# Fourier mixing and an MLP mixer in one kernel: second sine table turned ahead of stage one, last carried products ahead of the first token layer, the first chunk's residual added in PSUM

## Chip, core and metric

The kernel runs on one core of a Trainium2 chip. The time is the device time of one execution in microseconds (us); several executions are timed and the median is quoted. A profile is of one further or one of these executions, on the hardware profiler, and its span is about 1.8 us shorter than the time of the same run. Engines: PE is TensorE's matmul, PEld its weight load, DVE VectorE, ACT ScalarE, POOL GpSimd, SP SyncE.

## The reference

```python
def _attn_ref(x):                       # x: (8, 3008, 256)
    X = np.fft.fft(x, axis=1)
    X = np.fft.fft(X, axis=2)
    return X.real.astype(np.float32)

def _moe_ref(x, w_tok1, w_tok2, w_ch1, w_ch2):
    xt = x.transpose(0, 2, 1)
    h = np.maximum(xt @ w_tok1, 0.0) @ w_tok2       # the token layer, 256 hidden
    u = x + h.transpose(0, 2, 1)                    # the token residual
    h2 = np.maximum(u @ w_ch1, 0.0) @ w_ch2         # the channel layer, 1536 hidden
    return (u + h2).astype(np.float32)

# reference: _moe_ref(_attn_ref(x), ...)
```

## The kernel before

The kernel makes sine tables, transforms batch 0 in a setup ("head") of some 33 us, and then runs a software pipeline over eight batches of six chunks of 512 tokens. Each chunk has four quarter-chunks ("subs"). In a quarter-chunk PE does three channel products `pc` (from `ut` and `wc1`), parts of the next batch's transform and token layer, and a quarter of the second channel layer of the chunk before (`px`, `py`, or `po` in plain chunks). DVE runs its instructions in program order here, so a wait of one instruction holds those behind it: the residual that stands behind the fold (explained below) in DVE's queue began at 47.12 us in the profile of before.

The head's order, with the parts that the change touches (cuts are marked `# ...`):

```python
    warm(24)
    table3(tq, vq, (shift0[:], shift1[:]))
    turn(tp, tts_p, 16)                     # 12 PE transposes, 2 ACT copies, 16 filler products
    table_d()
    pieces = fold0()
    take(pieces, 5)
    own = zw0()                             # stage one and two of batch 0
    take(own, 2)
    turn_rows(tts_p, 1.0, 0)
    # ...
    turned_out(tts_q, turn_in(tq))          # the second table turned, in the middle of stage one/two
    for g2, e in enumerate((1, 1)):
        carried(tts_p, hp, g2, e)           # hp, hq: w_tok1 carried through the transform
    # ...
    mirrored(state[0]["w"], ps_any("pt1"))
    own = front(0)
    carried(tts_q, hq, 1, 1)
    take(own, 1)                            # third(0): writes yt, the transform's chunk 0
    carried(tts_q, hq, 2, 0)
    take(own, 1)                            # token layer, part 0, both halves
    carried(tts_q, hq, 3, 1, ps_mm)
    carried(tts_q, hq, 4, 0, ps_mm)
    carried(tts_q, hq, 5, 0, ps_mm)
    take(own, 3)                            # token layer, part 1; then pu of chunk 0, two halves
    tables_folded()
    filler(12)
    load_wc2()
    if BB > 1:
        x_tiles[1] = load_x(1)              # xp (plain loads) and xm (two gathers) of batch 1
    early = fold(1, [nc.vector] * 4)
```

The token layer of batch 0 and the residual of a chunk:

```python
            pts = [ps_out("pt1") for _ in range(2)]
            for th in range(2):
                tok1(pts[th], th, 0)
            yield
            sqs = []
            for th in range(2):
                tok1(pts[th], th, 1)
                sqs.append(part_q(pts[th]))              # ACT copy
            uvs = [units(pts[th], sqs[th]) for th in range(2)]   # DVE: a copy, a subtract, an add
            relu(0, uvs[0], (0,))
            # ...
            for h in range(2):                           # per chunk
                # ... pu = two products of w_tok2 with uu
                nc.vector.tensor_tensor(
                    out=ut[:, h, 0:n].rearrange("p (a b) -> p a b", b=64),
                    in0=pu[:, 0:n].rearrange("p (b a) -> p a b", b=64),
                    in1=y.rearrange("p (a b) -> p a b", b=64), op=AT.add)
```

In the steady loop, batch 1's fold (DVE, reads `xm`) is taken early, in six quarter-chunks of batch 0, from the last one of the first chunk to the first one of the third:

```python
                take(own, own_plan[b > 0][sub])
                # ...
                if b == 0 and sub == 4:
                    weight_sums()                        # DVE, needs wc2
                # ...
                if b == 0 and 3 <= sub < 9:
                    take(early, 2)
                    if sub == 8:
                        x_tiles[2] = load_x(2)
```

## Time and profile before

| | before |
|---|---|
| time, median of the first three runs | 607.27 us (607.20 to 607.56) |
| span of the profile | 605.8 us |
| PE busy | 589.6 us, 97% |
| first channel product | at 32.91 us |
| gather of batch 1's xm seen by DVE | at 45.68 us |
| PE standing on DVE's `sb` and `osb` near 58 us | 1.20 us and 0.25 us |

From the page of the kernel before: the span; the line of busy us, share of the span and number of instructions; and the granted clock in tenths, in 40 equal slices.

```profile
span 605.8 us, 15712 instructions
...
PE 589.6 (97%) x6323; PEld 421.7 (70%) x6323; DVE 454.3 (75%) x1022; ACT 437.0 (72%) x983; POOL 148.5 (25%) x234
...
PEclk9999999999999999999999999999999999999999
```

The table of busy time by stretch of the kernel before; its columns are the stretch, its length, and for PE, PEld, DVE, ACT and POOL the busy us with the number of instructions, then the granted clock, the DMA share and GB/s.

```profile
33.00:45.60 12.60, 12.60 (x76) 6.44 (x74) 7.15 (x12) 9.66 (x18) 0.00 (x0) 1.00 1.21 173
45.60:59.20 13.60, 12.40 (x95) 7.96 (x94) 13.28 (x30) 8.53 (x16) 0.51 (x2) 1.00 0.54 107
...
100.00:300.00 200.00, 200.00 (x2148) 142.09 (x2146) 154.65 (x332) 146.92 (x336) 49.03 (x73) 1.00 0.49 90
300.00:580.00 280.00, 280.00 (x3048) 200.43 (x3046) 207.40 (x449) 202.25 (x462) 59.40 (x92) 1.00 0.40 79
```

The clock was granted in full (1.00 in every stretch shown). From 100 us on PE is busy in every microsecond (200.00 of 200 us, then 280.00 of 280). So what happens earlier should do little more than move the moment at which this stretch begins. Between 45.6 and 59.2 us it is DVE that is full (13.28 of 13.60 us), and PE is not.

The chain of waits of the first 60 us of the kernel before, in order of time (start, us, what):

```profile
6.20 7.65 DMA w1p<-in_moe_w_tok_dram
...
14.14 13.87 DMA w2s<-in_moe_w_tok_dram
...
30.12 15.43 DMA xm<-in_x_dram,ix
...
45.68 0.24 DVE xp L455
...
58.66 0.47 DVE sb L753
```

After its first 6 us this chain doesn't pass through the head's compute at all. It runs from load to load (a DMA line's duration is the time from its issue to its landing) to the gather of xm for batch 1, then through DVE.

The timeline of DVE (start, us, engine, line, operation, out<-in, form, and in brackets the idle time before it with what ended it), kernel before:

```profile
41.33 0.68 DVE L704 TENSOR_TENSOR ut<-pu,yt 128x512 f16<-128x512 f32 x1
45.68 0.23 DVE L455 TENSOR_TENSOR xp<-xp,xm 94x16 f16<-94x16 f16 x1 [3.67 <-DMA xm<-in_x_dram,ix]
...
58.58 0.54 DVE L753 TENSOR_TENSOR sb<-c 128x768 f16<-128x768 f16 x1
```

DVE finished a residual at 42.0 us and then stood 3.67 us on the gather, because the fold comes next in its queue. From then on it works without a break up to the `sb` at 58.58.

The timeline of PE, kernel before, same columns:

```profile
31.07 1.33 PE L696 MATMUL pu<-w2s,uu 128*128 128x512 f16 x4 [0.73 <-ACT uu L627]
32.24 0.83 PE L298 MATMUL filler<-ident 128*128 128x128 f16 x12
32.91 1.58 PE L736 MATMUL pc<-ut,wc1p 128*128 128x512 f16 x6
...
57.65 0.33 PE L777 MATMUL py<-wst,sb 128*128 128x128 f16 x3
59.18 0.68 PE L777 MATMUL py<-wst,sb 128*128 128x128 f16 x9 [1.20 <-DVE sb L753]
60.10 0.83 PE L777 MATMUL px<-wst,sb 128*128 128x128 f16 x12 [0.25 <-DVE osb L762]
```

The first three lines are the end of the head: the products `pu`, twelve fillers while DVE adds the residual, the first channel product. The last three show PE waiting for DVE's `sb` and `osb` near 58 us.

### The profile page before, as it was taken

How to read it: one execution, taken by the hardware profiler on the slowest of the kernel's cores; microseconds unless marked ns; L12 is line 12 of the kernel's file. 1: busy time of each engine (PE TensorE's matmuls, PEld its weight loads, DVE VectorE, ACT ScalarE, POOL GpSimd, SP SyncE). 2: the span in 40 equal slices, each digit the busy share in tenths (PEclk: the TensorE clock that was granted, in tenths of full speed). 3: DMA queues.
4: the chain of work that ended last, by engine and by line, in shares of the span. 5: the costliest groups of instructions: out<-in, count | busy, mean ns of one | idle time of the engine just before them, and what ended most of it. 6: DMA issues, size and time to landing. Idle time of an engine off the chain costs nothing.

```text
span 605.8 us, 15712 instructions
## 1 busy us (share of the span) xinstructions
PE 589.6 (97%) x6323; PEld 421.7 (70%) x6323; DVE 454.3 (75%) x1022; ACT 437.0 (72%) x983; POOL 148.5 (25%) x234
## 2 busy tenths in 40 slices
PE   5999999999999999999999999999999999999996
PEld 3855667666777677666777677766777677766675
DVE  8759699559886698667988689755979666766672
ACT  8775986777677767677767777677776877767772
POOL 7600414112242131402223211411221112111131
PEclk9999999999999999999999999999999999999999
DMA  9995945643457223662519332492231424242423
GB/s 152 210 177 117 176 62 97 141 62 63 53 107 155 57 54 88 134 88 54 97 44 178 70 80 63 83 173 53 54 85 44 86 53 88 55 70 62 87 60 99
DMA packets 86665, 56.53 MB, mean 93 GB/s; under 512 B 54928, under 2 KB 83536, under 8 KB 85840
## 3 DMA queue, kind: packets, MB, share of 16 engines
q1 hardware_dynamic: 78048, 37.84, 32.5%
q0 software_dynamic: 8320, 17.49, 16.9%
q8 instruction: 49, 0.80, 0.5%
q14 instruction: 24, 0.20, 0.1%
q10 hardware_dynamic: 224, 0.20, 0.1%
HBM read 34.98 MB, written 24.64 MB: 98 GB/s over the span
## 4 chain that ended last, share of the span: by engine, by line
PE 86%; DMA 6%; DVE 5%; issue 1%; ACT 1%; POOL 1%; DVEq 0%; POOLq 0%
PE pc L736 37%; PE px L777 23%; PE py L777 9%; PE pu L696 6%; PE po L834 3%; PE pt L604 3%; DMA xm<-in_x_dram,ix 3%; DMA w2s<-in_moe_w_tok_dram 2%; PE pz L509 1%; DMA w1p<-in_moe_w_tok_dram 1%; DVE sb L753 1%; PE pq L636 1%; PE py L636 1%; DVE osb L762 1%; DVE xp L457 1%
## 5 line engine op out<-in xcount | busy, mean ns | idle before, releaser
L739 ACT ACTIVATE c<-pc 128x512 f16<-128x512 f32 (+1 forms) x572 | 295.8, 593 | 38.2 <-PE pc L736 20.6
L762 POOL TENSOR_TENSOR osb<-osb,rt 128x256 f32<-128x256 f32 x84 | 81.2, 966 | 375.6 <-DVE osb L762 359.9
L736 PE MATMUL pc<-ut,wc1p 128*128 128x512 f16 x576 | 140.5, 379 | 0.0
L777 PEld LDWEIGHTS <-c 128*128 128x128 f16 x2016 | 121.4, 98 | 20.7 <-issue 1.3
L736 PE MATMUL pc<-ut,wc1m 128*128 128x512 f16 (+1 forms) x576 | 134.8, 370 | 0.0
L704 DVE TENSOR_TENSOR ut<-pu,yt 128x512 f16<-128x512 f32 (+1 forms) x96 | 64.7, 674 | 52.7 <-PE pu L696 52.7
L777 PEld LDWEIGHTS <-sb 128*128 128x128 f16 x1512 | 89.9, 98 | 12.5 <-DVE sb L753 2.1
L782 ACT ACTIVATE m<-px 128x256 f32<-128x256 f32 x126 | 48.6, 386 | 68.6 <-PE px L777 43.1
L736 PEld LDWEIGHTS <-wc1p 128*128 128x128 f16 x576 | 52.2, 98 | 49.1 <-issue 2.6
L736 PEld LDWEIGHTS <-wc1m 128*128 128x128 f16 x576 | 53.0, 98 | 46.4
L777 PE MATMUL px<-wst,c 128*128 128x128 f16 x1008 | 70.8, 219 | 0.2 <-DVE c L753 0.2
L777 PE MATMUL px<-wc,c 128*128 128x128 f16 x1008 | 63.1, 219 | 0.0
L753 DVE TENSOR_TENSOR sb<-sb,c 128x768 f16<-128x768 f16 x84 | 50.3, 599 | 2.9
L305 ACT ACTIVATE z<-pz 128x480 f16<-128x480 f32 (+1 forms) x60 | 40.0, 671 | 16.9 <-PE pz L509 11.0
L753 DVE TENSOR_TENSOR sb<-c 128x768 f16<-128x768 f16 x84 | 49.8, 592 | 2.3 <-ACT c L739 2.3
L762 DVE TENSOR_TENSOR osb<-py,m 128x256 f32<-128x256 f32 x84 | 35.2, 419 | 20.8 <-ACT m L782 18.9
L696 PE MATMUL pu<-w2p,uu 128*128 128x512 f16 (+1 forms) x168 | 50.0, 379 | 0.0
L753 DVE TENSOR_TENSOR sb<-c,sb 128x768 f16<-128x768 f16 x84 | 47.2, 561 | 0.0
L753 DVE TENSOR_TENSOR c<-c 128x768 f16<-128x768 f16 x84 | 46.6, 555 | 0.0
L590 DVE SCALAR_TENSOR_TENSOR w<-alt,pw 128x131 f16<-128x131 f16 x84 | 29.3, 350 | 18.2 <-ACT w L305 17.6
L643 DVE TENSOR_TENSOR yt<-py,qs 128x512 f16<-128x512 f32 x48 | 30.9, 686 | 15.7 <-ACT qs L639 14.8
L777 PE MATMUL py<-wst,sb 128*128 128x128 f16 x504 | 35.3, 219 | 1.7 <-DVE sb L753 1.7
(184 smaller groups left out, 681.0 us busy)
## 6 DMA issues: line engine op xcount, KB each, us to landing
out_dram<-osb SPq DMA_DIRECT2D x83, 256.0 KB, 3.7
xp<-in_x_dram POOLq DMA_DIRECT2D x16, 272.0 KB
out_dram<-osb SPq DMA_DIRECT2D x11, 192.0 KB, 3.2
xp<-in_x_dram POOLq DMA_DIRECT2D x16, 127.5 KB
rt<-ut SPq DMA_TRANSPOSE x96, 3.6
w2s<-in_moe_w_tok_dram POOLq DMA_DIRECT2D x1, 1504.0 KB
w1p<-in_moe_w_tok_dram POOLq DMA_DIRECT2D x4, 192.0 KB
wc<-in_moe_w_ch_dram POOLq DMA_DIRECT2D x1, 768.0 KB
```

The source lines that it names most:

```text
L305: nc.scalar.activation(out=out_, in_=in_, func=AFT.Copy)
L590: nc.vector.scalar_tensor_tensor(out=w[:, g, 0:131], in0=alt[:], scalar=pw[:, 131:132], in1=pw[:, 0:131], op0=AT.mult, op1=AT.add)
L604: nc.tensor.matmul(pt[:, o:o + n], lhsT=hw[:, g, th * P:th * P + P], rhs=w[:, g, f:f + n], start=(g == 0), stop=(g == NG - 1))
L643: nc.vector.tensor_tensor(out=yt[:, h, CW * c:CW * c + CW], in0=py[:], in1=qs[:], op=op)
L696: nc.tensor.matmul(pu[:, 0:n], lhsT=uu[:, th, int(minus), h, :], rhs=w2_cols(b, c)[:, th], start=(th == 0), stop=(th == 1))
L704: nc.vector.tensor_tensor(out=ut[:, h, 0:n].rearrange("p (a b) -> p a b", b=64), in0=pu[:, 0:n].rearrange("p (b a) -> p a b", b=64), in1=y ...
L736: nc.tensor.matmul(pc[:, 0:n], lhsT=wc[:, h, ct * P:(ct + 1) * P], rhs=ut[:, h, 0:n], start=(h == 0), stop=(h == 1))
L739: nc.scalar.activation(out=c1[:, ct, 0:n], in_=pc[:, 0:n], func=AFT.Relu)
L753: nc.vector.tensor_tensor(out=o, in0=x, in1=y, op=op)
L762: eng.tensor_tensor(out=o, in0=x, in1=y, op=AT.add)
L777: nc.tensor.matmul(o[:, t], lhsT=a(k)[:, f:f + P], rhs=w(k), start=(first and t == 0 and k == 0), stop=(k == HC - 1), skip_group_check=True)
L782: nc.scalar.activation(out=m[:, i], in_=pa[:, 0], func=AFT.Copy)
```

## The change

Its intent is to bring the first channel product forward. The second table `tq` is turned in idle time before stage one (its two PSUM buffers are held meanwhile, so the ring gives only the others); the last four carried products run in a row ahead of the token layer; the token layer's first part is copied out of PSUM early; and for the first chunk the residual is put into PSUM by a product with the identity, so that the two halves can be copied out by DVE and ACT side by side.

```diff
-    turn(tp, tts_p, 16)
+    held.add("o2")
+    turned_out(tts_p, turn_in(tp, ps_mm))
+    filler(12)
+    pts_q = turn_in(tq, ps_out)
+    filler(4)
 ...
-    turned_out(tts_q, turn_in(tq))
+    turned_out(tts_q, pts_q)
+    held.clear()
 ...
-    carried(tts_q, hq, 2, 0)
-    take(own, 1)
-    carried(tts_q, hq, 3, 1, ps_mm)
-    carried(tts_q, hq, 4, 0, ps_mm)
-    carried(tts_q, hq, 5, 0, ps_mm)
+    for g2, e in ((2, 0), (3, 0), (4, 1), (5, 0)):
+        carried(tts_q, hq, g2, e)
     take(own, 3)
     tables_folded()
-    filler(12)
 ... token layer of batch 0:
+                pt = ps_out("pt1")
+                tok1(pt, th, 0)
+                sp = perb.tile([P, 130], FP32, tag="sp", name="sp", bufs=2)
+                nc.scalar.activation(out=sp[:], in_=pt[:, 0:130], func=AFT.Copy)
 ...
+                for h, op in ((0, AT.subtract), (1, AT.add)):
+                    nc.vector.tensor_tensor(out=uvs[th][:, h, 1:P], in0=sps[th][:, 2:129],
+                                            in1=pt[:, 130:257], op=op)
 ... first chunk:
+            if (b, c) == (0, 0):
+                pus = [ps_f("pu") for _ in range(2)]
+                for h in range(2):
+                    nc.tensor.matmul(pus[h][:], lhsT=ident[:],
+                                     rhs=yt[:, h, 0:CW].rearrange("p (a b) -> p b a", b=64),
+                                     start=True, stop=False)
+                # ... the four products of w_tok2 with uu, accumulated
+                for h in range(2):
+                    copy(1 - h, ut[:, h, :].rearrange("p (a b) -> p a b", b=64),
+                         pus[h][:].rearrange("p (b a) -> p a b", b=64))
```

More of the change, by code (lines that the diff above doesn't have):

```diff
@@ L65, with ps_mm, ps_out @@
         tc.tile_pool(name="psump", bufs=1, space=bass.MemoryType.PSUM))
-    def ps_mm(name):
-        return psum.tile([P, 512], FP32, tag="mm", name=name, bufs=3)
-    def ps_out(name):
-        return psum.tile([P, 512], FP32, tag="o2", name=name, bufs=2)
+    def ps_mm(name, dt=FP32, n=512):
+        return psum.tile([P, n], dt, tag="mm", name=name, bufs=3)
+    def ps_out(name, dt=FP32, n=512):
+        return psum.tile([P, n], dt, tag="o2", name=name, bufs=2)
     def ps_f(name, dt=FP32, n=512):
@@ L77 @@
                   ("o2", 2)))
+    held = set()
     def ps_any(name, dt=FP32, n=512):
-        tag, bufs = next(ring)
+        tag, bufs = next(r for r in ring if r[0] not in held)
         return psum.tile([P, n], dt, tag=tag, name=name, bufs=bufs)
@@ L256, in turned, with turn_in @@
                 for _ in range(2)]
-    def turn_in(tab):
+    def turn_in(tab, pool=ps_any):
         pts = []
         for h in range(2):
-            pt = ps_any("pt", FP16, 1024)
+            pt = pool("pt", FP16, 1024)
             for g in range(6):
@@ L662, in rest @@
             yield
-            pts = [ps_out("pt1") for _ in range(2)]
+            uvs, sps = [], []
             for th in range(2):
-                tok1(pts[th], th, 0)
+                pt = ps_out("pt1")
+                tok1(pt, th, 0)
+                sp = perb.tile([P, 130], FP32, tag="sp", name="sp", bufs=2)
+                nc.scalar.activation(out=sp[:], in_=pt[:, 0:130], func=AFT.Copy)
+                uv = perb.tile([P, 2, P], FP32, tag="uv", name="uv", bufs=2)
+                nc.vector.tensor_copy(out=uv[:, :, 0], in_=sp[:, 0:130:129])
+                sps.append(sp)
+                uvs.append(uv)
             yield
-            sqs = []
             for th in range(2):
-                tok1(pts[th], th, 1)
-                sqs.append(part_q(pts[th]))
-            uvs = [units(pts[th], sqs[th]) for th in range(2)]
-            relu(0, uvs[0], (0,))
-            for h in range(2):
-                nc.scalar.activation(out=uu[:, 1, 0, h, :], in_=uvs[1][:, h, :],
-                                     func=AFT.Relu)
+                pt = ps_mm("pt1")
+                tok1(pt, th, 1)
+                for h, op in ((0, AT.subtract), (1, AT.add)):
+                    nc.vector.tensor_tensor(out=uvs[th][:, h, 1:P], in0=sps[th][:, 2:129],
+                                            in1=pt[:, 130:257], op=op)
             for th in range(2):
-                relu(th, uvs[th], (1, 2))
+                for h in range(2):
+                    nc.scalar.activation(out=uu[:, th, 0, h, :], in_=uvs[th][:, h, :],
+                                         func=AFT.Relu)
             yield
@@ L691, in rest @@
             uts.append(ut)
+            if (b, c) == (0, 0):
[4 more added lines that the diff above has]
+                                     start=True, stop=False)
+                for th in range(2):
+                    for h in range(2):
+                        nc.tensor.matmul(pus[h][:], lhsT=uu[:, th, 0, h, :],
+                                         rhs=w2_cols(b, c)[:, th],
+                                         start=False, stop=(th == 1))
+                for h in range(2):
+                    copy(1 - h, ut[:, h, :].rearrange("p (a b) -> p a b", b=64),
+                         pus[h][:].rearrange("p (b a) -> p a b", b=64))
+                for th in range(2):
+                    relu(th, uvs[th], (1, 2))
+                yield
+                continue
             for h in range(2):
```

## The prediction

> **What bounds the kernel.** The page shows a span of 605.8 us, TensorE (PE) busy 97%, DVE 75%, ACT 72%. The table of busy time by stretch shows PE at 200.0 of 200 us from 100 to 300 us and 280 of 280 from 300 to 580. All edits act before 35 us, so any gain is an earlier arrival at that steady stretch.
>
> The timeline of PE from 10 to 33 us shows dense setup with small gaps (1.17 us in stage one, 0.34 us, 0.73 us before pu, then twelve fillers under a wait). But the chain of waits for the first 60 us runs through the loads: w1p, w2s (13.87 us), then the gather of xm for batch 1 (15.43 us, landing 45.55), then back-to-back DVE work to 59 us. DVE's timeline shows it idle 3.67 us until that gather lands, because batch 1's early fold stands in its queue; from 45.6 to 59.2 it is busy 13.28 of 13.60 us. PE then stands 1.20 us on DVE's sb (57.98 to 59.18). So PE's position at 59 us is set by the load queue plus 13.6 us of DVE.
>
> **What the change does.**
> - tq turned early: replaces four of sixteen fillers and idle time; takes 12 transposes (0.83 us busy) out of the stretch at 16.8 us. But the next stage also needs z, whose DVE copy ends at 18.03: 0 to 0.2 us gained. Six PSUM buffers instead of eight for stage one: 0 to 0.2 us back.
> - Last four carried products together, ahead of the token layer: no work saved, waits hidden.
> - Token layer: the first part is copied out early, so after its last product DVE does two short adds a unit.
> - Residual in PSUM: two identity matmuls (0.22 us each) added; two serial DVE adds (0.6 us apart) become a DVE and an ACT copy in parallel. The twelve fillers at 32.2 us go.
>
> Worked out from these durations, ut is complete near 31.9 us instead of 33.2: 1.1 to 1.4 us locally.
>
> **How much is on the critical path.** Almost nothing. First wall: the order of instructions shows that the second weight load of the first channel product waits for the gathered half of wc1p, whose last piece lands at 32.76 us, against 32.91 for that product's start before. Only 0.2 to 0.4 us is realised there. Second wall: the xm gather at 45.55 us. Its issue order on POOL doesn't change and DMA runs near 200 GB/s throughout, so it lands when it did; DVE waits longer, PE's stand at 58 us grows by what the head gained, and everything after is as before.
>
> The transposing loads of u start up to 0.8 us earlier. [...] both queues being active from 36 to 43 us. So the landing may move some tenths either way, which passes to the total one for one.
>
> **Prediction: 607.2 us, 8 in 10 between 606.4 and 607.8.** Faster by over 2%: 0.01; within 2%: 0.985; slower by over 2%: 0.005.
>
> **What would show it.** Right: ut written by about 32 us; the first channel product's second matmul still near 32.8; DVE idle before the fold about 4 us; the gather landing at 45.2 to 46; PE's resume on sb at 59 to 59.5; from 100 us on an unchanged timeline shifted by under 0.6 us. Wrong: PE resuming on sb before 58.8, or the landing a microsecond off.
>
> **What would make it wrong.** The gather landing up to an estimated 1 us earlier or later because the transposing loads mix differently; a longer stage one; DVE's run after the fold shortening.

## The result, and the profile after

| | before | after |
|---|---|---|
| median of four runs each | 607.24 us | 607.25 us |
| the four runs | 607.56, 607.27, 607.20, 606.57 | 606.68, 607.89, 607.74, 606.77 |
| ratio, 95% interval | | 1.0002, 0.9985 to 1.0019 |
| span of the profile | 605.8 us | 604.9 us |

Ratios are the mean time of one kernel's runs over that of the other's of the same rounds, so not quite the ratio of the medians quoted. The time is the same. But the runs of the kernel after fall into two pairs about 1 us apart, and its profile is of a run from the lower one. That has to be explained before the equal medians can be believed.

The same views of the kernel after. Its page:

```profile
span 604.9 us, 15690 instructions
...
PE 590.5 (98%) x6313; PEld 421.0 (70%) x6313; DVE 453.2 (75%) x1021; ACT 437.3 (72%) x985; POOL 147.7 (24%) x234
...
PEclk9999999999999999999999999999999999999999
```

Its table of busy time by stretch:

```profile
33.00:45.60 12.60, 12.15 (x73) 6.43 (x73) 8.91 (x17) 10.42 (x22) 0.20 (x1) 1.00 1.17 210
45.60:59.20 13.60, 13.60 (x114) 9.03 (x113) 13.43 (x29) 8.94 (x17) 2.02 (x2) 1.00 0.38 102
```

PE now works 13.60 of 13.60 us in the second stretch, where it lost 1.2 us before; in the first stretch it lost 0.45 us, where it lost none.

Its chain of waits from 40 to 62 us:

```profile
57.70 0.52 PE pu L722 x2
58.22 0.67 PE py L803 x12
58.89 0.67 PE px L803 x12
```

In this run the chain is on PE, and the gather isn't in it. Its timeline of DVE:

```profile
41.74 0.68 DVE L730 TENSOR_TENSOR ut<-pu,yt 128x512 f16<-128x512 f32 x1
43.97 0.23 DVE L457 TENSOR_TENSOR xp<-xp,xm 94x16 f16<-94x16 f16 x1 [1.54 <-DMA xm<-in_x_dram,ix]
...
56.84 0.54 DVE L779 TENSOR_TENSOR sb<-c 128x768 f16<-128x768 f16 x1
```

The gather was seen at 43.97 us, 1.71 us earlier than in the profile of before; DVE stood 1.54 us. The run from the fold to `sb` is as long as before (12.87 against 12.90 us from start to start). Its timeline of PE:

```profile
30.00 1.88 PE L703 MATMUL pu<-yt,ident 128*128 128x512 f16 x2
31.70 1.23 PE L708 MATMUL pu<-w2s,uu 128*128 128x512 f16 x4
33.45 1.46 PE L762 MATMUL pc<-ut,wc1p 128*128 128x512 f16 x6 [0.52 <-DVE ut L305]
...
58.06 0.83 PE L803 MATMUL py<-wst,sb 128*128 128x128 f16 x12
58.73 0.83 PE L803 MATMUL px<-wst,sb 128*128 128x128 f16 x12
```

Here is the surprise in the head. The two identity products start at 30.00 and the next product only at 31.70, where two such products of 512 columns were expected to take about 0.44 us. The first channel product starts at 33.45, 0.54 us later than before. Near 58 us PE has no wait left: `px<-wst,sb` begins at 58.73, against 60.10 before, and it does so because the gather landed early in this run.

So two questions were open. Does the landing of the gather follow from the change, or is it luck? And what is the head's true place worth?

### The profile page after: what moved, and what is told of

It reads as the page before. It is cut to its first block, busy times and chain, and to the rows that moved or that the text cites. A ratio compares the mean times of both kernels' runs of the same rounds, so it can differ in the third digit from the quotient of the medians.

```text
span 604.9 us, 15690 instructions
## 1 busy us (share of the span) xinstructions
PE 590.5 (98%) x6313; PEld 421.0 (70%) x6313; DVE 453.2 (75%) x1021; ACT 437.3 (72%) x985; POOL 147.7 (24%) x234
## 4 chain that ended last, share of the span: by engine, by line
PE 92%; DVE 4%; ACT 3%; issue 0%; DVEq 0%; POOL 0%; POOLq 0%
PE pc L762 39%; PE px L803 23%; PE py L803 9%; PE pu L722 7%; PE po L860 4%; PE pt L606 4%; PE pz L511 1%; PE pq L638 1%; PE py L638 1%; DVE sb L779 1%; PE pw L590 1%; PE pw L589 1%; DVE osb L788 1%; DVE w L592 1%; ACT c L765 0%
## 5 line engine op out<-in xcount | busy, mean ns | idle before, releaser
L788 POOL TENSOR_TENSOR osb<-osb,rt 128x256 f32<-128x256 f32 x84 | 79.9, 951 | 377.6 <-DVE osb L788 361.1
L730 DVE TENSOR_TENSOR ut<-pu,yt 128x512 f16<-128x512 f32 (+1 forms) x94 | 63.4, 674 | 52.1 <-PE pu L722 52.1
L779 DVE TENSOR_TENSOR sb<-c 128x768 f16<-128x768 f16 x84 | 48.3, 575 | 2.4 <-ACT c L765 2.4
```

The source lines that it names most:

```text
L730: nc.vector.tensor_tensor(out=ut[:, h, 0:n].rearrange("p (a b) -> p a b", b=64), in0=pu[:, 0:n].rearrange("p (b a) -> p a b", b=64), in1=y ...
L779: nc.vector.tensor_tensor(out=o, in0=x, in1=y, op=op)
L788: eng.tensor_tensor(out=o, in0=x, in1=y, op=AT.add)
```

## The experiments

The theory: PE reaches `px<-wst,sb` near 58 us at the later of two times, its own pace (set by the head) and DVE's (set by the landing of the gather). The change made the head slower, through strided identity products, and the landing varies from run to run whatever the kernel. The rivals: the wait near 58 us is a symptom of something else; the change gains as intended; the transposing loads of `u`, which the change moves, decide the landing.

All twelve kernels were run with five rounds (e7 has six runs), in three sets, each on another chip. The first four kernels shared nine runs of the kernel before (median 606.57, 606.10 to 607.53), the next four eleven (606.25, 606.05 to 607.09), the last four nine (606.65, 606.08 to 607.21).

### e1: the kernel before with the fold a quarter-chunk later

```diff
-                if b == 0 and 3 <= sub < 9:
+                if b == 0 and 4 <= sub < 10:
                     take(early, 2)
-                    if sub == 8:
+                    if sub == 9:
```

> Kernel before, with the fold of batch 1 taken one quarter-chunk later, so that DVE does the weight sums before it stands on the xm gather. Wall theory (TensorE's place at 59 us is set by the landing of that gather plus 13.6 us of DVE): TensorE no longer stands before py<-wst,sb near 58 us (1.20 + 0.25 us in the profile of before), and the time falls by 1.0 to 1.8 us against before, to about 605.7, with less spread from run to run. Rival (the stand is a symptom, TensorE is late for some other reason): the stand only moves, time unchanged within 0.3 us.

Measured: 605.74 us (605.68 to 605.92), ratio 0.9986 (0.9972 to 1.0000). The spread fell from 1.4 to 0.24 us. PE's timeline in its profile, at the place where before stood:

```profile
57.64 0.83 PE L777 MATMUL py<-wst,sb 128*128 128x128 f16 x12
58.31 0.83 PE L777 MATMUL px<-wst,sb 128*128 128x128 f16 x12
```

No wait is left, although nothing in the head was touched. All five runs lie below all nine of before, though the interval just reaches 1. The gain of 0.8 us between medians is under the 1.0 to 1.8 us expected; presumably the gather lands early in many runs of the kernel before, which have little to gain (the one profile of before is of a late one). This profile also gives the pace of before's head when nothing holds it: `px<-wst,sb` at 58.31 us.

### e2: the kernel after with the same later fold

The edit is that of e1, on the kernel after.

> Kernel after, with the same later fold. With the wall gone the true place of the head counts. Theory (the two identity products take about 0.86 us each instead of 0.22 because they read yt with a 128-byte stride, so the head is 0.2 to 0.5 us later than before's): 0.2 to 0.5 us slower than e1. Rival (the change gains its 0.2 to 0.4 us in the head, as predicted): 0.2 to 0.4 us faster than e1.

Measured: 606.61 us (606.53 to 606.61), 0.87 us above e1, both with little spread. With the gather out of the way the change costs time, more than expected. PE's timeline in its profile:

```profile
58.74 0.83 PE L803 MATMUL px<-wst,sb 128*128 128x128 f16 x12
```

That is 0.43 us after e1's, and it is the head. The lag then grows to 0.78 us at 240 us and 0.93 us at 430 us. The cause of this growth was not found, but the traces place most of it: between 214 and 261 us the lag over e1 (by the starts of ACT's `m<-px`) grows by 0.32 to 0.35 us in each of the five profiles with the identity products (after, e2, e3, e9, e10), with a wait of 0.21 or 0.22 us of PE on DVE's `osb` near 241 us, and by 0.06 us at most in the eight others, without that wait. So about half of what the change costs here is not the head's place. The part near 241 us goes with the residual in PSUM, whatever its stride (e4, e7, e11 and e12 keep the rest of the change and don't show it); why it comes so late stays open.

### e3: the permutation on the identity product's output

```diff
-                    nc.tensor.matmul(pus[h][:], lhsT=ident[:],
-                                     rhs=yt[:, h, 0:CW].rearrange("p (a b) -> p b a", b=64),
+                    nc.tensor.matmul(pus[h][:].rearrange("p (b a) -> p a b", b=64),
+                                     lhsT=ident[:],
+                                     rhs=yt[:, h, 0:CW].rearrange("p (a b) -> p a b", b=64),
```

The later fold of e1 was kept, here and in e4.

> As e2, but the identity product reads yt contiguously and the permutation is on its PSUM output. Stride theory: the pair falls from about 1.7 us to 0.45 us of issue, ut is written near 32.2 us, the first channel product's second matmul starts when wc1p's gathered half has landed (31.9 to 32.8 us), and the time is 0.6 to 1.2 us under e2. Rival A (identity products are slow for another reason, or a strided PSUM write costs as much): the pair still takes over 1.2 us and the time equals e2.

Measured: 606.03 us (605.66 to 606.21), 0.58 us under e2, just short of the 0.6 to 1.2 us expected. PE's timeline in its profile:

```profile
30.43 1.02 PE L703 MATMUL pu<-yt,ident 128*128 128x512 f16 x2
31.25 1.25 PE L709 MATMUL pu<-w2s,uu 128*128 128x512 f16 x4
```

The pair takes 0.82 us from its start to the next product's, 0.41 us each: half of e2's and the kernel after's 0.85, but not 0.22: neither the 0.45 us forecast for the pair nor the rival's 1.2 us came out. A read with a stride of 128 bytes is the larger part of the cost; a PSUM write with a stride of 32 bytes costs too (0.41 us against 0.215 without a stride in e10). (The whole head was late in this profile: the third stage's first product came at 25.39 us, against 24.96 in the kernel after.)

### e10: the identity product without any stride

```diff
-                                     rhs=yt[:, h, 0:CW].rearrange("p (a b) -> p b a", b=64),
+                                     rhs=yt[:, h, 0:CW],
```

The later fold of e1 was kept. The residual lands on wrong tokens, so the output is wrong (relative error 0.16).

> e2 with the identity products reading yt in its stored order and writing PSUM in its stored order; the first chunk's residual lands on wrong tokens, so the result is wrong on purpose. It measures the identity product without any stride. Theory (the predicted 0.22 us holds for a contiguous read): 0.2 to 0.25 us each by the start of the next product, ut written about 1.2 us earlier than in e2, time as e3 or up to 0.4 us below, about 605.5. Rival (an identity product costs more than any other 512-column product whatever its stride): over 0.4 us each, time as e3 or above.

Measured: 605.48 us (605.30 to 605.60), ratio 0.9983 (0.9970 to 0.9997), 1.13 us under e2's median of other rounds. PE's timeline:

```profile
30.08 0.59 PE L703 MATMUL pu<-yt,ident 128*128 128x512 f16 x2
30.51 1.21 PE L708 MATMUL pu<-w2s,uu 128*128 128x512 f16 x4
```

0.43 us for the pair, 0.215 us each. So the whole excess time of the change's identity products is their access pattern: 0.215 us contiguous, 0.41 with a strided write, 0.85 with a strided read. DVE begins to write `ut` at 31.50 us here, against 32.70 in the kernel after. Not all of the lead is kept: against e1 this profile is 0.79 us ahead at `px<-wst,sb` near 58 us and 0.21 us ahead at 430 us. Of the 0.58 us lost, 0.33 us is the growth near 241 us told under e2; the rest was not traced.

### e4: the change without the residual in PSUM

```diff
-                for h in range(2):
-                    nc.tensor.matmul(pus[h][:], lhsT=ident[:], ...)
 ...
-                                         start=False, stop=(th == 1))
+                                         start=(th == 0), stop=(th == 1))
 ...
-                    copy(1 - h, ut[:, h, :]..., pus[h][:]...)
+                    nc.vector.tensor_tensor(out=ut[:, h, :]..., in0=pus[h][:]...,
+                                            in1=yt[:, h, 0:CW]..., op=AT.add)
```

> As e2, with the residual of the first chunk added by DVE as before and no identity products; all else of the change stays. If the identity products are what cost the head: 0.2 to 0.7 us faster than e2 and 0 to 0.4 us faster than e1 (two serial DVE adds are back, 0.6 us apart). If the other parts of the change (buffers held, products moved, token layer split) cost: no faster than e1.

Measured: 605.55 us (605.34 to 606.62), 1.06 us under e2 and 0.19 us under e1 by medians. PE's timeline:

```profile
30.23 1.37 PE L704 MATMUL pu<-w2s,uu 128*128 128x512 f16 x4
32.12 0.38 PE L761 MATMUL pc<-ut,wc1p 128*128 128x512 f16 x1 [0.52 <-DVE ut L708]
32.95 1.25 PE L761 MATMUL pc<-ut,wc1p 128*128 128x512 f16 x5 [0.46 <-DMA wc1p<-in_moe_w_ch_dram,ixc]
```

The rest of the change does what it was meant to do: `pu` begins at 30.23 us, 0.84 us earlier than before. But the second matmul of the first channel product then waits 0.46 us for the gathered half of `wc1p`. This is the first wall that the prediction named, seen in the open. Two of the five runs are higher (606.31 and 606.62). In the profile, of a run at 605.55, DVE still stood 0.99 us on the xm gather in spite of the later fold; whether that was longer in the two higher runs isn't known, as they have no profile.

### e5 and e6: a head that is late on purpose

```diff
-    filler(12)
+    filler(36)
```

e5 has this in the kernel before, e6 in e1.

> Kernel before with 24 more filler products ahead of the first channel product (0.056 us each: TensorE's head 1.0 to 1.3 us later), nothing else. Wall theory: TensorE has 0.4 to 1.8 us of standing before sb near 58 us to give, depending on when the xm gather lands, so most of it is swallowed: the time rises by 0 to 0.6 us, and the stand near 58 us shrinks by what the head lost. Rival (no wall, TensorE's own work sets the time): plus 1.0 to 1.3 us.

> The same 24 fillers on e1, where the fold no longer stands in DVE's way. Wall theory: nothing is left to swallow them, so 1.0 to 1.3 us over e1, about 606.9. Rival: whatever e5 showed, the same here.

Measured: e5 607.25 us (607.14 to 608.65), 1.00 us above before in the same rounds; e6 607.30 us (607.05 to 608.22). e6 is somewhat above what was expected, 1.56 us over e1 by medians of different rounds and 1.20 us at `px<-wst,sb` (59.51 against 58.31). e5 went against the theory as it was put: 0 to 0.6 us had been expected, and both medians are nearer to the rivals (1.0 to 1.3 us for e5; e6 the same as e5). The profile of e5, of its lowest run, shows why:

```profile
44.64 0.23 DVE L455 TENSOR_TENSOR xp<-xp,xm 94x16 f16<-94x16 f16 x1 [1.41 <-DMA xm<-in_x_dram,ix]
59.54 0.83 PE L777 MATMUL px<-wst,sb 128*128 128x128 f16 x12
```

In that run the gather was seen by DVE at 44.64 us, so DVE could serve PE at about 59.0 us, and PE itself arrived at 59.54. In runs with an early gather there is little standing to give, and a later head is paid for. The wall is not always the later of the two arrivals.

### e7: e4's head with the fold in its old place

> e4 with the fold back in its old place: the head is the best one measured (first channel product's last five matmuls from 32.95 us), but DVE again stands on the xm gather. Wall theory: its gain is swallowed, time within 0.3 us of before in the same rounds, with before's spread, and TensorE stands 1 to 2.2 us before sb near 58 us. Rival: keeps e4's gain, about 605.6.

Measured: 607.01 us (605.80 to 609.40; the six runs are 609.40, 605.80, 607.20, 609.13, 606.63, 606.82), ratio 1.0012 (0.9997 to 1.0027). The best correct head, measured at 605.55 us in e4, gains nothing here: its median is 0.76 us above before's of the same rounds, more than the 0.3 us expected. Two runs are much slower than before's slowest, which had not been expected either; the mean of the four others, 606.61 us, is still not below before's 606.39. The profile is of the run at 609.40. PE's timeline there:

```profile
59.25 0.68 PE L802 MATMUL py<-wst,sb 128*128 128x128 f16 x9 [1.66 <-DVE sb L778]
60.18 0.83 PE L802 MATMUL px<-wst,sb 128*128 128x128 f16 x12 [0.25 <-DVE osb L787]
60.84 2.69 PE L761 MATMUL pc<-ut,wc1p 128*128 128x512 f16 x6
```

The gather was late (DVE saw it at 45.76 us), and because the head was early PE stood 1.66 us, more than in the profile of before. Six channel products then took 2.69 us in place of 1.46. The table of busy time by stretch for the same kernel has the reason in the column after POOL's:

```profile
60.00:62.00 2.00, 1.82 (x15) 1.07 (x15) 2.00 (x5) 0.96 (x2) 1.15 (x2) 0.73 0.87 200
62.00:64.00 2.00, 2.00 (x12) 1.13 (x11) 0.93 (x2) 1.66 (x4) 1.81 (x4) 0.50 1.00 135
64.00:66.00 2.00, 2.00 (x23) 1.41 (x21) 0.69 (x2) 1.77 (x5) 1.58 (x2) 0.92 0.90 174
```

The granted clock fell: the trace's clock record shows half clock for 3.41 us from 60.9 us on. This cost another 1.66 us (the lag against e1 is 1.87 us at `px<-wst,sb` near 60 us and 3.53 us at the next one, near 74 us). PE's longest single stand before it was 1.66 us; in the 3.41 us up to the fall (57.50 to 60.91 us) it stood 1.91 us in all. The profile of before, with stands of 1.20 and 0.25 us, kept its clock (1.00 from 56 to 66 us). That the stands caused the fall is an inference from one profile. The clock records of e7 are 51.20, 3.41 and 542.72 us long, all whole multiples of 3.413 us; what sets these lengths is not shown. The other high run (609.13) has a mean clock of 0.996, the four others 0.998 to 1.0. But a run of e12 (606.63 us) has 0.995, and in e12's profile, of another run, PE doesn't stand near 58 us; so what makes the clock fall stays open.

### e8: the transposing loads of u held back

```diff
+                if b == 0 and sub == 3:
+                    u0 = state[0]["ut"][0]
+                    for h in range(2):
+                        copy(0, u0[0:1, h, 0:1], u0[0:1, h, 0:1])
+                    box["rt"] = turn_u(0, 0)
+                    turned_u[0, 1] = turn_u(0, 1)
```

The two earlier calls for these chunks are taken out.

> Kernel before, with the four transposing loads of u's first two chunks held back (a one-element copy of u onto itself on ScalarE after the first chunk's last relu, about 43 us) so that they no longer overlap the xm gather. Theory [...]: the gather lands by 44.0 us in the profile, DVE starts the fold by 44.1, TensorE stands under 0.5 us before sb, and the times are 606.0 to 606.5 with little spread. Rival (the landing's spread comes from the load queue itself): landing and spread as before, 606.1 to 607.6.

Measured: 606.10 us (605.89 to 606.90), ratio 0.9997 (0.9984 to 1.0010). The loads began at 40.69 us instead of 32.74, earlier than meant. DVE saw the gather at 44.49 us, and the spread of the times stayed at 1.0 us. So taking the transposing loads out of 8 us of the gather's way did not take the spread away, and in the one profile the gather landed no earlier than in the early ones of kernels that kept these loads in place. The expected 44.1 us and the narrow band were missed; the rival fits better. One landing more speaks against the theory that these loads decide. The trace's records of completed transfers give, for each profile, when the last piece of wc1p's gather landed and when the last piece of batch 1's xm gather landed:

| kernel | wc1p gather, us | xm gather, us |
|---|---|---|
| e10 | 31.82 | 44.17 |
| after | 31.94 | 43.85 |
| e5 | 31.96 | 44.52 |
| e2 | 31.96 | 44.19 |
| e12 | 32.07 | 44.66 |
| e8 | 32.18 | 44.37 |
| e1 | 32.20 | 44.19 |
| e9 | 32.55 | 45.55 |
| e6 | 32.64 | 45.62 |
| e7 | 32.72 | 45.63 |
| before | 32.76 | 45.56 |
| e4 | 32.90 | 46.09 |
| e11 | 32.92 | 46.26 |
| e3 | 33.24 | 45.84 |

The transposing loads moved their first packet at 36.1 us or later in every one of these profiles, so they cannot have delayed the first of the two landings. The profiles fall into two groups without an overlap. Where the xm gather will be late, the gather of wc1p is already late by 0.35 us or more at 32 us. The kernel after (after, e9) and small edits of both kernels are found in either group, so the landing is a property of the run and not of this change.

The traces show two things more. The lateness at 32 us is mostly that of one completion: the trace records up to sixteen completions for one load, and in six of the seven late profiles the one before the last came at 31.77 to 32.12 us, as in the early ones (31.72 to 32.11), and only the last one 0.80 to 1.16 us after it (0.06 to 0.37 us in the early ones; in e9 the last two came late together). And it is older than batch 1's loads: a load of `w1p`, issued at 7.6 us, had landed by 14.78 to 15.47 us in the early profiles and by 15.57 to 16.63 us in the late ones; POOL issued the gather of wc1p 0.76 or 0.77 us after that landing in all fourteen. The gap between these groups is only 0.1 us, and what holds up a load's last completion stays open.

### e9: the kernel after once more

> The changed kernel once more, with more rounds. Theory (TensorE reaches px<-wst,sb near 58 us at the later of its own pace and 14.4 us after DVE starts the fold; its own pace is 0.42 us later than before's): runs in which the xm gather lands early are 0.4 to 0.7 us slower than before's early ones (606.6 to 606.8 against 606.1 to 606.3), runs in which it lands late are as slow as before's late ones; the mean ratio is 1.0000 to 1.0010. Rival (the change is neutral): same lowest time as before within 0.2 us.

Measured: 607.02 us (608.11, 606.74, 606.91, 607.02, 607.14), ratio 1.0008 (0.9994 to 1.0021). The lowest run is 0.66 us above before's lowest of the same rounds (606.08). The ratio is as the theory had it, but the interval still contains 1, so within these rounds the slowdown isn't separated from noise. Over all rounds, the lowest of nine runs of the kernel after is 606.68 us, and 21 of 33 runs of the kernel before are faster than that; but 20 of the 33 come from rounds and chips in which the kernel after did not run. Round by round the means differ by 0.12 us (first four against four) and 0.62 us (here), and neither is clear of the noise. The profile, of the run at 608.11, has both the late gather, in DVE's timeline,

```profile
45.67 0.23 DVE L457 TENSOR_TENSOR xp<-xp,xm 94x16 f16<-94x16 f16 x1 [2.56 <-DMA xm<-in_x_dram,ix]
```

and PE standing on DVE again, in PE's timeline:

```profile
58.75 1.07 PE L803 MATMUL py<-wst,sb 128*128 128x128 f16 x12
60.07 0.83 PE L803 MATMUL px<-wst,sb 128*128 128x128 f16 x12 [0.25 <-DVE osb L788]
```

So the wait that the profile of after didn't show comes back with the late gather.

### e11 and e12: the best order found

e11 is e4 with the fold from the sixth quarter-chunk on, three pieces at a time. e12 is e11 with `tq` turned where it was before.

```diff
-                if b == 0 and 3 <= sub < 9:
-                    take(early, 2)
+                if b == 0 and 5 <= sub < 9:
+                    take(early, 3)
```

> e4 with the fold still later (four quarter-chunks of three pieces, from the sixth quarter-chunk on), so that DVE does not stand on the gather even when it lands at 46 us. Wall theory: e4's two slow runs (606.3, 606.6) go, all runs at 605.3 to 605.6, 0.2 to 0.4 us under e1. Rival: e4's slow runs had another cause, and the spread stays.

> e11 with tq turned where it was before and all eight PSUM buffers in stage one. The profiles show TensorE at the third stage's first product at 24.96 us with the early turn and 24.89 without, so the early turn is worth nothing: within 0.15 us of e11. Rival (the early turn gains its 0 to 0.2 us): 0.1 to 0.3 us slower than e11.

Measured: e11 605.66 us (605.54 to 606.40), ratio 0.9989 (0.9975 to 1.0003); e12 605.46 us (605.33 to 606.63), ratio 0.9991 (0.9977 to 1.0005). Both have occasional higher runs left, so the later fold did not cure e4's spread, as the rival of e11 said; the profiles of both show PE without a wait near 58 us and a gather that DVE no longer meets. The early turn of `tq` is worth nothing: e12 is no slower than e11, and the third stage's first product is at 24.88 us in e12, 25.00 in e11, 24.89 before and 24.96 after. e12 has the lowest median of the correct kernels, but e1, e4, e11 and e12 are within 0.3 us of each other, and the intervals against before reach 1 in all four, so by these intervals none is a proven gain. Only e1 has every run below all of before's of its rounds (605.92 at most, 606.10 at least).

### The rule, checked

In the profiles whose fold is in its old place, the distance from DVE's fold to PE's `px<-wst,sb` is 14.4 us wherever PE stood (before: 60.10 - 45.68 = 14.42). The rule "the later of fold + 14.42 and the head's own pace" then gives:

| kernel | fold begins | fold + 14.42 | own pace (from) | measured |
|---|---|---|---|---|
| before | 45.68 | 60.10 | 58.31 (e1) | 60.10 |
| after | 43.97 | 58.39 | 58.74 (e2) | 58.73 |
| e5 | 44.64 | 59.06 | 59.51 (e6) | 59.54 |
| e7 | 45.76 | 60.18 | 58.02 (e4) | 60.18 |
| e8 | 44.49 | 58.91 | 58.31 (e1) | 58.88 |
| e9 | 45.67 | 60.09 | 59.43 (e2, its head 0.69 late) | 60.07 |

The 14.42 was fitted on before alone. All other rows agree within 0.03 us. (e9's own pace is e2's plus the 0.69 us by which its third stage began later, 25.65 against 24.96 us.)

## Why the prediction was right or wrong

- **The time** (607.2 forecast, 607.25 measured, range 606.4 to 607.8): held. The equality to 0.01 us was chance, as four runs a kernel cannot settle less than the 1 us between runs. There was luck in the range too: the reason given (the wait swallows a head that gained) is not what the profile of after shows, where the head lost time and an early gather left no wait. By the prediction's own test ("Wrong: PE resuming on sb before 58.8, or the landing a microsecond off") that profile counts against it: PE began `py<-wst,sb` at 58.06 us, and the gather landed at 43.85 us in place of 45.55.
- **"Almost nothing" on the critical path, because of the xm gather**: right for runs with a late gather, shown by e1 (the wait vanishes with the fold moved), by e7 (the best correct head gains nothing with the fold in its place) and by the 14.42 us rule. Too strong for runs with an early gather, where PE's own pace counts (after, e5).
- **"It lands when it did"**: wrong as a statement about a run. It lands between 43.85 and 46.26 us, whatever the kernel. This also is why "DVE idle before the fold about 4 us" and "PE's resume on sb at 59 to 59.5" were not seen in the profile of after, where they are 1.54 us and no wait. (Its premise, DMA "near 200 GB/s throughout", holds to 40 us, with 194 to 216 GB/s from 8 us on in the trace of before; from 40 to 44 us it has 167 GB/s.)
- **"Two identity matmuls (0.22 us each)"**: the term that was mis-sized. They take 0.85 us each with the strided read (e10 shows 0.215 without a stride). So `ut` was not "complete near 31.9 us" but near 33.6 (ACT's half 32.97 + 0.60), and the head did not gain 0.2 to 0.4 us but lost 0.43 us (e2 against e1). A stride of 128 bytes in the SBUF read cost a factor of four (0.85 us in after against 0.215 in e10), one of 32 bytes in the PSUM write a factor of 1.9 (0.41 us in e3). The product had been costed from its column count alone.
- **The first wall, the gathered half of wc1p**: the mechanism was right (e4, 0.46 us), but the kernel after never met it, as its first channel product comes at 33.45 us and the gather had landed at 31.94.
- **"An unchanged timeline" from 100 us on**: nearly. Shifts of 0.5 to 0.6 us against e1 appear after 100 us in e2 and e10, 0.33 to 0.35 us of it near 241 us in the kernels with identity products only.
- **tq early, 0 to 0.2 us**: nothing (e12 against e11).
- **The transposing loads moving the landing**: not found. Both queues were active from 36 to 43 us (in the trace of before 326 packets on the queue of the gathers and 615 on that of the transposing loads). These loads started 0.79 us later, not earlier (33.53 against 32.74 us), and e8 with the load table rules them out as the main cause.

## What to carry to other kernels

A gain ahead of a wait is worth only what the later of two arrivals leaves of it; move the waiting instruction behind work that doesn't need the data before shortening the other side, as a two-line shift of the fold gave 0.8 us here (by medians, with an interval that just reaches 1) and the whole rearranged head none. Cost a matmul by its access pattern as well as by its columns: the identity product here took 0.215 us without a permutation, 0.41 with one on its output and 0.85 with one on its input. And when two medians agree to 0.01 us but the runs of one kernel lie 1 us apart, look for what parts them before explaining the equality.
